# A feed-forward block whose four first products run ahead of its second products, with two PSUM banks taking turns

## The chip, the cores and the metric

The kernel runs on one core of a Trainium2 chip. A core has five engines with a queue of instructions each, worked off in order: TensorE (PE) multiplies matrices and writes to PSUM, VectorE (DVE), ScalarE (ACT) and GpSimd (POOL) work on elements, and SyncE (SP) issues DMA transfers. The metric is the device time of one execution in microseconds (us). Three timed runs of the kernel before took 1249.03, 1254.1 and 1255.2 us, the median is 1254.1. The profiled execution took 1257.39 us.

## The reference

Three stages, one after the other, on 4 batches of 576 tokens (2304 in all):

```
scores = q @ k.T / 8                          # 8 heads of 64, 576 keys
scores below a row's 32nd largest -> -1e9;  attn = softmax(scores);  x = attn @ v
h = x @ w_in                                  # 512 -> 2048
g = where(h > 0, h, exp(min(h, 0)) - 1);      x = g @ w_out        # 2048 -> 512
expert = argmax(cosine(x, expert_emb) / tau);  gate = its softmax weight
out = gate * (relu(x @ w1[expert]) @ w2[expert])                   # 8 experts, 512 -> 1024 -> 512
```

## The kernel before, in words

Numbers that need more than 16 bits are held as a high and a low half, so most products are three matmuls: high by high, high by low, low by high.

**Attention.** One tile is 128 queries of one head against 576 keys; four heads of the leftover 64 queries of a batch go in tiles of both heads together, so there are 144 tiles. PE makes the scores (line 781) into one of two score buffers of two PSUM banks each, ACT copies them out (787), DVE finds the threshold (676 to 708), ACT (691, 806, 818) and POOL (816, 821, 825) mask, exponentiate and split, SP transposes two tiles by DMA (827), and PE multiplies by v (857).

**Feed-forward.** After eight tiles 128 tokens are complete, which is a slot; there are 18. `norm_ops` divides by the sums, splits into two halves (`xs`, 889 to 895) and transposes by DMA to `xt`. `ffn_ops` then works in four units. A unit has a first product of 48 matmuls (`f1`, lines 916 to 918) into the PSUM bank `hp`; ACT takes exp and a clipped line of it (938, 939), DVE combines them with `hp` (940), and this is the last reader of the bank; ACT or POOL makes the high half `gt[0]` (945 or 943) and POOL the low half (946). The unit's second product is 12 matmuls of 512 columns (`f2`, 923 to 925) that add onto the PSUM bank `y`. Both products are issued in quarters (`K["cut"]` is 4), one operation of the planner each. When all four units have been added, `route_ops` takes `y` out of PSUM (962), turns it, finds the expert and its place in a list (966 to 1019), and writes the row to memory for the experts.

**Order.** A planner (`Plan`) writes the queues. Each operation has an engine, a supposed duration and a due time in tiles; an engine that is free takes, of the operations that can start, the one due first. The queue of each engine is fixed by this when the program is built. `Ring` hands out a set of buffers in turn, and a buffer is given again when the last user of its former holder is done. So with one `hp` bank the first product of unit 1 stands behind line 940 of unit 0. Eight PSUM banks are in use: `misc`, `sc` with four, `hp`, `y`, `acc`. There are two `gt` buffers and three `rr` buffers; `wl` is a 4 KB piece per partition through which the last of the feed-forward weights are prepared, and it is idle after that.

**Afterwards** the first expert's products on 128 early tokens start with the same two banks (`first_expert`), and then the experts run one by one behind a branch on a flag that all engines take.

Of the kernel before, what the change touches and what calls it, by code (L numbers as in the profile page):

```python
# [8 lines left out]
F32 = mybir.dt.float32  # L9
# [17 lines left out]
SC0 = 224  # L27

ENDS = (0, 83, 166, 248, 330, 412, 494, 576)
K = {'WD': 2.5, 'wa': 0.7, 'ws': 6.0, 'wsa': 0.6, 'wo': 6.0, 'wos': 13.0, 'wsp': (1, 1, 1, 1, 1, 1, 1, 1, 0, 0, 0, 0, 0, 0, 0, 0), 'kd': 5, 'qd': 7, 'vs': 1.3, 'va': 0.25, 'vp': -5.0, 'u': 20, 'cut': 4, 'ff0': 7, 'ffd': 7.0, 'rr': 3, 'nj': (3, 1), 'big': 3, 'kt': 4, 'wt': 0.4, 'wf': 0.9, 'vpo': 0, 'gth': 2, 'a4': (0, 20, 1), 'hp': 2, 'yb': 1, 'sc': 3, 'xt': 2, 'xsp': 0, 's': 5, 'w': 1, 'gt': 2, 'qraw': 1, 'dsc': 3.5, 'dcp': 2.0, 'dsg': 0.2, 'drl': 1.0, 'de': 1.0, 'dex': 0.8, 'dhi': 0.8, 'dlo': 0.9, 'dav': 3.5, 'dno': 3.5, 'drt': 2.0, 'f3': 0.3, 'f6': 0.6, 'f9': 0.9, 'f15': 2.4, 'ffs': 0.0, 'ct': 0.4, 'we': 0, 'wd0': -2.9, 'ahead': 4}  # L30


def pick(n, key):
# [156 lines left out]
def topk_attention_ffn_experts_kernel(  # L190
# [91 lines left out]
    def ring(pool, shape, dt, name, bufs):  # L282
        return Ring(bufs, lambda: pool.tile(shape, dt, name=name, bufs=bufs))
# [67 lines left out]
    def attention_and_ffn(fast):  # L351
# [30 lines left out]
        r_misc = ring(ps, [128, 512], F32, "misc", 1)  # L382

        r_sc = ring(ps, [128, 1024], F32, "sc", 2)
        r_h = ring(ps, [128, 512], F32, "hp", 1)
        r_y = ring(ps, [128, DM], F32, "y", K["yb"])
        r_acc = ring(ps, [128, DM], F32, "acc", 1)
        r_kraw = rings(raw, 2, ([128, NJ, 2, D], F32, "kraw"), ([64, 2, D], F32, "krawl"))
        r_vraw = rings(raw, 1, ([128, 2, NJ, D], F32, "vraw"), ([64, 2, D], F32, "vrawl"))
# [19 lines left out]
        r_xl = ring(at, [128, 2, DM], F16, "xl", 1)  # L409
        r_xt = ring(ff, [128, 2, KB, 128], F16, "xt", K["xt"])  # L410
        r_rr = ring(ff, [128, 512], F32, "rr", K["rr"])
        r_gt = ring(ff, [128, 2, 4, 128], F16, "gt", K["gt"])
        r_big = ring(ff, [128, 2 * S], F32, "big", K["big"])
        r_rt = rings(sm, 2, ([128, 5], F32, "ss"), ([128, 6, E], F32, "L"), ([128, 9], BF, "oh"), ([128, 2], I32, "pos"))
        r_pw = ring(sm, [128, 4], F32, "pw", 1)

        for r in [r_sc, r_s, r_k, r_php, r_pt, r_top, r_w, r_acc, r_xs, r_xt, r_h, r_gt, r_y]:
            r.in_order = True
        b_const = Buf(t=ident)
        b_sv, b_sw, b_so, b_sc3 = Buf(t=sv), Buf(t=sw), Buf(t=so), Buf(t=sc3)  # L420
# [78 lines left out]
        def w_split(t, tb, i, sb, due, pool):  # L499
            hi, lo, f = (wview(t, i, x) for x in range(3))  # L500
            s = sb.t[:, 0:1]
            if pool == 2:
                op("act", 1040, due, lambda: nc.scalar.activation(f, f, AF.Copy, scale=s), r=[sb], w=[tb[i + 1]])
                op("pool", 1105, due, lambda: nc.gpsimd.tensor_scalar(hi, f, 1.0, 0.0, op0=ALU.mult, op1=ALU.add), r=[tb[i + 1]], w=[tb[i]])
                op("pool", 2300, due, lambda: nc.gpsimd.tensor_tensor(lo, f, hi, op=ALU.subtract), r=[tb[i + 1]], w=[tb[i]])
                return
            op("act", 1040, due, lambda: nc.scalar.activation(hi, f, AF.Copy, scale=s), r=[tb[i + 1], sb], w=[tb[i]])
            if pool:
                op("act", 1040, due, lambda: nc.scalar.activation(f, f, AF.Copy, scale=s), r=[sb], w=[tb[i + 1]])
                op("pool", 2300, due, lambda: nc.gpsimd.tensor_tensor(lo, f, hi, op=ALU.subtract), r=[tb[i + 1]], w=[tb[i]])  # L510
                return
            op("dve", 1196, due, lambda: nc.vector.scalar_tensor_tensor(lo, f, s, hi, op0=ALU.mult, op1=ALU.subtract),
               r=[tb[i + 1], sb], w=[tb[i]])

        def wi_at(part, kb, fb):
            return wview(wi, fb // 2, part)[:, kb * 256 + (fb % 2) * 128:kb * 256 + (fb % 2) * 128 + 128]
# [2 lines left out]
            return wview(wo, fb // 2, part)[:, (fb % 2) * 512:(fb % 2) * 512 + 512]  # L519


        KT, VB, QT, hold = {}, {}, {}, []

        def thirds(x, m, first, due, dst, ns, reads):

# [88 lines left out]

        def get_q(b, j, due):
            n = 128 if j < NJ else SL
            x, m, qn, qd, qx = r_qraw(), (r_misc if QT else r_y)(), r_big(), r_qd(), Buf(t=1)
            QT[b, j] = qd
            op("sp", 750, due - 1.5, lambda: nc.sync.dma_start(x.t[:n], q[b, :, j * 128:j * 128 + n, :].rearrange("h p d -> p h d")),
               w=[x], lat=DLAT, after=hold if len(QT) > 1 else [])  # L620

            def part(i):
                return qn.t.bitcast(BF)[:, i * NP * 128:i * NP * 128 + NP * n]

            def tr():
                for p in range(NP):
                    turned(m.t[:, p * n:(p + 1) * n], x.t[:n, 2 * p:2 * p + 2, :].rearrange("p h d -> p (h d)"), n, p)

            def place():
                src = qn.t.bitcast(BF)[:, 0:3 * NP * 128].rearrange("p (i x) -> p i x", i=3)[:, :, 0:NP * n]  # L630
                for h in range(2):
                    rows = slice(64 * h, 64 * h + 64)
                    nc.sync.dma_start(qd.t[0:64, :, h, 0:NP * n], src[rows])
                    nc.sync.dma_start(qd.t[64:128, 0:2, h, 0:NP * n], src[rows, 0:2])
                    nc.sync.dma_start(qd.t[64:128, 2, h, 0:NP * n], src[rows, 0])

            op("pe", 430 if j < NJ else 270, due, tr, r=[x, b_const], w=[m, qn, qd])
            thirds(qx, m, NP * n, due - U, part, 478 if j < NJ else 290, [qn])
            op("sp", 2600, due - U, place, r=[qn, qx], w=[qd], lat=DLAT)
# [266 lines left out]


        def ffn_ops(c, d0, d1):
            xt, y = xts[c], r_y()

            def f1(hp, f, i0, i1):
                for i in range(i0, i1):
                    fb = 4 * f + i
                    for kb in range(KB):
                        xh, xl = (xt.t[:, x, kb, :] for x in range(2))
                        nc.tensor.matmul(hp.t[:, i * 128:i * 128 + 128], wi_at(0, kb, fb), xh, start=(kb == 0), stop=False)  # L916
                        nc.tensor.matmul(hp.t[:, i * 128:i * 128 + 128], wi_at(0, kb, fb), xl, start=False, stop=False)  # L917
                        nc.tensor.matmul(hp.t[:, i * 128:i * 128 + 128], wi_at(1, kb, fb), xh, start=False, stop=(kb == KB - 1))  # L918

            def f2(gt, f, i0, i1):  # L920
                for i in range(i0, i1):
                    fb = 4 * f + i
                    nc.tensor.matmul(y.t, gt.t[:, 0, i, :], wo_at(0, fb), start=(fb == 0), stop=False)  # L923
                    nc.tensor.matmul(y.t, gt.t[:, 0, i, :], wo_at(1, fb), start=False, stop=False)  # L924
                    nc.tensor.matmul(y.t, gt.t[:, 1, i, :], wo_at(0, fb), start=False, stop=(fb == NFB - 1))  # L925

            def unit(f):
                d = d0 + (d1 - d0) * f / (NFB // 4)
                hp, r, gt = r_h(), r_rr(), r_gt()
                n = 4 // K["cut"]  # L930

                def v3(x):
                    return x.rearrange("p (a b) -> p a b", a=4)

                for i in range(0, 4, n):
                    op("pe", 660 * n, d, lambda i=i: f1(hp, f, i, i + n), r=[xt] + wi_b[2 * f + i // 2:2 * f + (i + n + 1) // 2], w=[hp])

                op("act", 571, d + K["f3"], lambda: nc.scalar.activation(r.t, hp.t, AF.Exp, scale=sc3[:, 0:1]), r=[hp, b_sc3], w=[r])
                op("act", 707, d + K["f3"], lambda: nc.scalar.activation(r.t, r.t, AF.Relu, scale=sc3[:, 4:5], bias=sc3[:, 1:2]), r=[b_sc3], w=[r])
                op("dve", 720, d + K["f6"], lambda: nc.vector.scalar_tensor_tensor(r.t, hp.t, sc3[:, 2:3], r.t, op0=ALU.mult, op1=ALU.min),  # L940
                   r=[hp, b_sc3], w=[r])
                if (4 * c + f) * K["gth"] % 8 < K["gth"]:
                    op("pool", 588, d + K["f9"], lambda: nc.gpsimd.tensor_scalar(gt.t[:, 0], v3(r.t), 1.0, 0.0, op0=ALU.mult, op1=ALU.add), r=[r], w=[gt])
                else:
                    op("act", 520, d + K["f9"], lambda: nc.scalar.activation(gt.t[:, 0], v3(r.t), AF.Copy), r=[r], w=[gt])  # L945
                op("pool", 1113, d + K["f9"], lambda: nc.gpsimd.tensor_tensor(gt.t[:, 1], v3(r.t), gt.t[:, 0], op=ALU.subtract), r=[r], w=[gt])  # L946
                for i in range(0, 4, n):
                    FIRST["last"] = op("pe", 645 * n, d + K["f15"], lambda i=i: f2(gt, f, i, i + n), r=[gt] + wo_b[2 * f + i // 2:2 * f + (i + n + 1) // 2], w=[y])

            for f in range(NFB // 4):  # L950
                unit(f)
            route_ops(c, y, d1 + K["drt"])
            if c == NSLOT - K["ahead"]:
                first_tokens(d1 + K["drt"] + 1)
# [80 lines left out]
        def first_expert():  # L1035
# [6 lines left out]
            op("pool", 275, N + 3, lambda: nc.gpsimd.tensor_scalar(gate0, g.t[:, DM:DM + 1], 1.0, 0.0, op0=ALU.mult, op1=ALU.add), r=[g], w=[b_ids])  # L1042
            op("pe", 860, N + 3, lambda: turn0(m.t, g.t), r=[g, b_const], w=[m])
            op("act", 478, N + 3, lambda: nc.scalar.activation(x0, m.t, AF.Copy), r=[m], w=[x], after=old)
            up0(op, N + 60, x0, x, [r_h(), r_y()], late(0, 1024), Buf(t=1), raw, after=[FIRST["last"]])


        def start_ops():
# [450 lines left out]
```

## Time and profile before

| | us |
|---|---|
| median of 3 runs | 1254.1 |
| profiled execution | 1257.39 |
| its span in the trace | 1255.6 |
| busy in the span: PE, DVE, ACT, POOL | 1036.1, 865.1, 847.8, 780.8 |
| feed-forward and attention end at about | 938 |

Matmuls overlap in the trace and their ends are modelled, so that PE's busy time is an upper bound of what it needs. The stretches differ: the first 200 us prepare the weights, the stretch to 856 us is attention and feed-forward side by side, the next 80 us are what is left of feed-forward, and the last 317 us are the experts. Idle time of an engine counts only where another waits for it, so a row on a wait has to be read with the stretch in which it falls.

### The profile page before, as it was taken

The page shows a single profiled execution, that of the slowest core. Times are in us where ns is not written, and L with a number is a line of the kernel's source. Part 1 is how long each engine was busy: PE and PEld are TensorE (multiplying, and loading weights), DVE is VectorE, ACT ScalarE, POOL GpSimd, SP SyncE. Part 2 cuts the span into 40 slices and gives each one's busy share as a digit, 9 for nine tenths or more (in the row PEclk, how much of TensorE's full clock was granted, in tenths as well). Part 3 has the DMA queues.
Part 4 walks back from the last instruction along what each step waited for, and adds up shares of the span by engine and source line. Part 5 has one row for each costly group of instructions (what it writes and reads, how often), then busy time and mean ns, then how long its engine had stood idle before and what let it go on. Part 6 is the DMA issues. An engine that isn't in the chain of part 4 may idle for free. (4 is left out here: it accounts for less than half of the span.)

```text
span 1255.6 us, 28591 instructions
## 1 busy us (share of the span) xinstructions
PE 1036.1 (83%) x10112; PEld 799.0 (64%) x10112; DVE 865.1 (69%) x3588; ACT 847.8 (68%) x1807; POOL 780.8 (62%) x816
## 2 busy tenths in 40 slices
PE   4565537899798999798898988998887788998996
PEld 2354426666566777576676666776664677777785
DVE  4789999988798988789887898886213244434310
ACT  3687878889788989878887888876233244444421
POOL 1267979887688988678886788988313234323300
PEclk9957757999899999989998988999898889999998
DMA  7997633746764757945756674434407455455400
GB/s 202 303 235 192 161 93 71 144 94 149 161 122 100 125 107 156 167 81 102 126 95 127 146 145 85 90 77 89 136 11 228 143 184 185 134 163 178 142 20 16
DMA packets 321732, 165.85 MB, mean 132 GB/s; under 512 B 257990, under 2 KB 298054, under 8 KB 321552
## 3 DMA queue, kind: packets, MB, share of 16 engines
q1 hardware_dynamic: 316816, 150.67, 52.1%
q0 software_dynamic: 4736, 12.92, 3.4%
q8 instruction: 95, 1.56, 0.6%
q14 instruction: 85, 0.70, 0.2%
HBM read 77.43 MB, written 11.40 MB: 71 GB/s over the span
## 5 line engine op out<-in xcount | busy, mean ns | idle before, releaser
L916 PE MATMUL hp<-xt,ww 128*128 128x128 f16 x1152 | 216.8, 229 | 25.0 <-DVE rr L940 22.8
L917 PE MATMUL hp<-xt,ww 128*128 128x128 f16 x1152 | 216.7, 229 | 0.0
L918 PE MATMUL hp<-xt,ww 128*128 128x128 f16 x1152 | 216.4, 229 | 0.0
L816 POOL TENSOR_TENSOR arena<-arena,k 128x576 f32<-128x576 f32 x144 | 191.4, 1330 | 37.6 <-ACT k L806 36.7
L825 POOL TENSOR_TENSOR php<-arena,php 128x576 f16<-128x576 f32 x144 | 188.0, 1306 | 6.5
L781 PE MATMUL sc<-arena_r,qd 128*128 128x288 bf16 (+1 forms) x960 | 145.5, 308 | 43.2 <-ACT arena L787 17.7
L676 DVE MAX8 cand<-arena 128x8 f32<-128x82 f32 (+1 forms) x1008 | 161.3, 229 | 26.1 <-ACT arena L787 25.2
L787 ACT ACTIVATE arena<-sc 128x288 f32<-128x288 f32 x288 | 113.5, 408 | 47.0 <-PE sc L781 45.4
L857 PEld LDWEIGHTS <-pt 128*128 128x128 f16 (+3 forms) x2400 | 99.7, 104 | 68.6 <-DMA pt<-php 36.3
L781 PEld LDWEIGHTS <-qd 128*128 128x128 bf16 (+1 forms) x960 | 86.7, 107 | 88.4 <-issue 44.7
L916 PEld LDWEIGHTS <-ww 128*128 128x128 f16 x1152 | 119.8, 104 | 27.1 <-DVE rr L940 15.3
L821 POOL TENSOR_SCALAR php<-arena 128x576 f16<-128x576 f32 x144 | 101.5, 705 | 47.4 <-ACT arena L818 44.3
L917 PEld LDWEIGHTS <-ww 128*128 128x128 f16 x1152 | 118.8, 103 | 17.1 <-issue 11.9
L691 ACT ACTIVATE k<-arena,mba 128x576 bf16<-128x576 f32 x144 | 111.4, 774 | 14.8 <-DVE mx L696 7.7
L806 ACT ACTIVATE k<-arena,mba 128x576 bf16<-128x576 f32 x144 | 111.7, 776 | 14.0 <-DVE mba L708 8.0
L818 ACT ACTIVATE arena<-arena,mx 128x576 f32<-128x576 f32 x144 | 111.6, 775 | 11.8 <-POOL arena L816 11.4
L918 PEld LDWEIGHTS <-ww 128*128 128x128 f16 x1152 | 119.0, 103 | 0.0
L857 PE MATMUL acc<-vb,pt 128*128 128x64 f16 (+1 forms) x1920 | 91.5, 201 | 32.7 <-DMA pt<-php 30.8
L925 PE MATMUL y<-ww,gt 128*128 128x512 f16 x288 | 109.2, 379 | 4.6 <-POOL gt L946 4.6
L707 DVE MAX8 w<-w 128x8 f32<-128x585 f32 x144 | 109.9, 763 | 4.1 <-POOL w L701 3.2
L923 PE MATMUL y<-ww,gt 128*128 128x512 f16 x288 | 109.5, 380 | 0.6 <-ACT gt L945 0.6
L924 PE MATMUL y<-ww,gt 128*128 128x512 f16 x288 | 109.1, 379 | 0.0
(300 smaller groups left out, 2747.1 us busy)
## 6 DMA issues: line engine op xcount, KB each, us to landing
arena<-in_moe_w_dram SPq DMA_DIRECT2D x52, 512.0 KB, 5.6
arena_r<-big SPq DMA_DIRECT2D x64, 144.0 KB, 2.6
big<-in_moe_w_out_dram SPq DMA_DIRECT2D x16, 512.0 KB, 4.6
ww<-in_moe_w_in_dram SPq DMA_DIRECT2D x14, 512.0 KB, 7.1
qd<-big SPq DMA_DIRECT2D x32, 192.0 KB, 2.9
ysc<-big SPq DMA_DIRECT2D x20, 258.0 KB, 4.8
w<-in_moe_w_dram SPq DMA_DIRECT2D x10, 512.0 KB, 12.4
big<-in_v_dram SPq DMA_DIRECT2D x9, 512.0 KB, 8.8
```

The costliest lines, as they stand in the source:

```text
L676: v.max(out=cand.t[:, 8 * g:8 * g + 8], in_=x()[:, ENDS[g]:ENDS[g + 1]])
L691: op("act", 760, n + K["dsg"], lambda: nc.scalar.activation(k.t(), x(), AF.Sign, scale=-1.0, bias=th.t, accum_out=ds.t), r=[sb, th, k.base ...
L781: nc.tensor.matmul(o[64 * g:64 * g + 64] if s is None else o, qd.t[:, i, g, p * n:p * n + n], kt.t[:, g, i // 2, cs], start=i == 0, stop=i ...
L787: op("act", 291, n - K["dcp"], lambda c=c: nc.scalar.activation(sb.t()[:, c * 288:c * 288 + 288], sc.t[:, SC0 + c * 288:SC0 + c * 288 + 28 ...
L806: op("act", 667, n + K["drl"], lambda: nc.scalar.activation(k.t(), sb.t(), AF.Relu, scale=-HUGE, bias=kb.t), r=[sb, kb, s2, k2], w=[k])
L816: op("pool", 1242, e, lambda sb_=sb_, k_=k_: nc.gpsimd.tensor_tensor(sb_.t(), sb_.t(), k_.t(), op=ALU.subtract), r=[k_, s2, k2], w=[sb_])
L818: op("act", 760, e + K["dex"], lambda sb_=sb_, mx_=mx_, i_=i_: nc.scalar.activation(sb_.t(), sb_.t(), AF.Exp, scale=scale, bias=mx_(), acc ...
L825: op("pool", 1270, e + K["dlo"], lambda sb_=sb_, i=i: nc.gpsimd.tensor_tensor(ph.t[:, i, 1, 0:S], sb_.t(), ph.t[:, i, 0, 0:S], op=ALU.subt ...
L857: nc.tensor.matmul(acc.t[out_, cs], t[h][rows, g, :], rhs, start=(i == 0), stop=(i == len(units) - 1))
L916: nc.tensor.matmul(hp.t[:, i * 128:i * 128 + 128], wi_at(0, kb, fb), xh, start=(kb == 0), stop=False)
L917: nc.tensor.matmul(hp.t[:, i * 128:i * 128 + 128], wi_at(0, kb, fb), xl, start=False, stop=False)
L918: nc.tensor.matmul(hp.t[:, i * 128:i * 128 + 128], wi_at(1, kb, fb), xh, start=False, stop=(kb == KB - 1))
```

## The change

The first products of a slot's four units are issued with their elementwise work; the four activation results are kept in four `gt` buffers, two of which lie in `wl`; and the second products of all four follow, due close to the end of the slot's time. `hp` and `y` become one ring of two banks: of the five buffers that a slot takes, four are first products and the fifth is `y`. The writers of `gt` also wait for the last of the weight preparation (`done`), since that uses `wl`.

```diff
-        r_h = ring(ps, [128, 512], F32, "hp", 1)
-        r_y = ring(ps, [128, DM], F32, "y", K["yb"])
+        r_h = ring(ps, [128, 512], F32, "hp", 2)
...
-        r_gt = ring(ff, [128, 2, 4, 128], F16, "gt", K["gt"])
+        gts = [ff.tile([128, 2, 4, 128], F16, name=f"gt{i}", bufs=1) for i in range(2)]
+        gts += [wl.bitcast(F16)[:, i * 1024:i * 1024 + 1024].rearrange("p (a b c) -> p a b c", a=2, b=4) for i in range(2)]
+        r_gt = turns(4, lambda i: gts[i])
...
-            op("dve", 1196, due, lambda: nc.vector.scalar_tensor_tensor(lo, f, s, hi, op0=ALU.mult, op1=ALU.subtract),
-               r=[tb[i + 1], sb], w=[tb[i]])
+            done[:] = [op("dve", 1196, due, lambda: nc.vector.scalar_tensor_tensor(lo, f, s, hi, op0=ALU.mult, op1=ALU.subtract),
+               r=[tb[i + 1], sb], w=[tb[i]])]
...
-            xt, y = xts[c], r_y()
+            xt, second = xts[c], []
...
-                    op("act", 520, d + K["f9"], lambda: nc.scalar.activation(gt.t[:, 0], v3(r.t), AF.Copy), r=[r], w=[gt])
+                    op("act", 520, d + K["f9"], lambda: nc.scalar.activation(gt.t[:, 0], v3(r.t), AF.Copy), r=[r], w=[gt], after=done)
...
-                for i in range(0, 4, n):
-                    FIRST["last"] = op("pe", 645 * n, d + K["f15"], lambda i=i: f2(gt, f, i, i + n), r=[gt] + wo_b[2 * f + i // 2:2 * f + (i + n + 1) // 2], w=[y])
+                second.append((gt, f))
...
             for f in range(NFB // 4):
                 unit(f)
+            y, n = r_h(), 4 // K["cut"]
+            for gt, f in second:
+                for i in range(0, 4, n):
+                    FIRST["last"] = op("pe", 645 * n, d1 + (f - 3) * .2, lambda gt=gt, f=f, i=i: f2(y, gt, f, i, i + n),
+                                       r=[gt] + wo_b[2 * f + i // 2:2 * f + (i + n + 1) // 2], w=[y])
             route_ops(c, y, d1 + K["drt"])
...
-            up0(op, N + 60, x0, x, [r_h(), r_y()], late(0, 1024), Buf(t=1), raw, after=[FIRST["last"]])
+            up0(op, N + 60, x0, x, [r_h(), r_h()], late(0, 1024), Buf(t=1), raw, after=[FIRST["last"]])
```

The planner's order changes with it on all engines. First, TensorE's queue in the last slot, from the end of unit 1's first product on. The numbers behind the names tell allocations apart; `hp_15497` is unit 1's bank and `gt_15495` unit 0's result. Before:

```order
16085 L918 MATMUL hp_15497<-xt_15398,ww_151 128x128
16086 L923 LDWEIGHTS gt_15495
16087 L923 MATMUL y_15547<-ww_151,gt_15495 128x512
16088 L924 LDWEIGHTS gt_15495
16089 L924 MATMUL y_15547<-ww_151,gt_15495 128x512
```

Unit 1's first product is followed by unit 0's second. Now (`hp_15425` is unit 1's bank, `hp_15479` unit 2's, line numbers are larger by three):

```order
16083 L920 MATMUL hp_15425<-xt_15360,ww_151 128x128
16084 L921 LDWEIGHTS ww_151
16085 L921 MATMUL hp_15425<-xt_15360,ww_151 128x128
16086 L919 LDWEIGHTS ww_151
16087 L919 MATMUL hp_15479<-xt_15360,ww_151 128x128
```

Unit 2's first product stands at that place, in the other bank of the ring, and all the second products stand behind unit 3's first.

Second, GpSimd's queue where the last pair of attention tiles is finished (821 and 825 make its halves, 946 is the low half of a feed-forward unit of the last slot but one, 869 the sums). Before:

```order
L821 TENSOR_SCALAR php_114<-arena 128x576
L943 TENSOR_SCALAR gt<-rr 128x512
L825 TENSOR_TENSOR php_114<-arena,php_114 128x576
L946 TENSOR_TENSOR gt<-rr,gt 128x512
L821 TENSOR_SCALAR php_114<-arena 128x576
L869 TENSOR_SCALAR rinv<-sums 128x8
L825 TENSOR_TENSOR php_114<-arena,php_114 128x576
```

Now (lines 824, 828, 949 and 872 are the same four):

```order
L949 TENSOR_TENSOR gt_157<-rr,gt_157 128x512
L824 TENSOR_SCALAR php_114<-arena 128x576
L949 TENSOR_TENSOR wl<-rr,wl 128x512
L828 TENSOR_TENSOR php_114<-arena,php_114 128x576
L872 TENSOR_SCALAR rinv<-sums 128x8
L824 TENSOR_SCALAR php_114<-arena 128x576
L949 TENSOR_TENSOR wl<-rr,wl 128x512
L828 TENSOR_TENSOR php_114<-arena,php_114 128x576
```

Before, one low half of that slot stood ahead of the last attention product; now all four do.

Third, ScalarE's queue in slot 9 (938 is the exp of a unit, 939 its line, 945 its high half; 787, 691, 806 and 818 are attention). Before, from the third unit's exp on:

```order
L938 ACTIVATE rr<-hp,sc_125 128x512
L691 ACTIVATE k,dsa<-arena,mba 128x576
L939 ACTIVATE rr<-rr,sc_125 128x512
L818 ACTIVATE arena,sums<-arena,mx 128x576
L787 ACTIVATE arena<-sc 128x288
L818 ACTIVATE arena,sums<-arena,mx 128x576
L787 ACTIVATE arena<-sc 128x288
L527 ACTIVATE big<-misc 128x512
L945 ACTIVATE gt<-rr 128x512
L806 ACTIVATE k<-arena,mba 128x576
L527 ACTIVATE big<-misc 128x512
L787 ACTIVATE arena<-sc 128x288
```

Now (lines 941, 942 and 948 are the exp, the line and the high half; 694, 790, 809, 821 attention):

```order
L941 ACTIVATE rr<-hp,sc_125 128x512
L694 ACTIVATE k,dsa<-arena,mba 128x576
L942 ACTIVATE rr<-rr,sc_125 128x512
L790 ACTIVATE arena<-sc 128x288 x2
L809 ACTIVATE k<-arena,mba 128x576
L941 ACTIVATE rr<-hp,sc_125 128x512
L694 ACTIVATE k,dsa<-arena,mba 128x576
L821 ACTIVATE arena,sums<-arena,mx 128x576
L948 ACTIVATE wl<-rr 128x512
L942 ACTIVATE rr<-rr,sc_125 128x512
```

The third and fourth exp of a slot have moved together: five instructions lie between them now, and fifteen before (three more than the rows show).

## Rows read from the trace of the kernel before

**Rows 1.** The page's first line: span and instructions.
```profile
span 1255.6 us, 28591 instructions
```

**Rows 2.** Windows: start:end, length, busy us (count) of PE, PEld, DVE, ACT, POOL; PEclk; DMA.
```profile
200.00:856.00 656.00, 591.82 (x6992) 439.93 (x6992) 568.86 (x2746) 558.43 (x1279) 537.27 (x602) 0.95 0.61 119
856.00:892.00 36.00, 32.56 (x392) 24.23 (x390) 16.17 (x57) 18.94 (x37) 24.64 (x31) 0.95 0.59 153
938.00:1255.00 317.00, 266.00 (x1512) 223.83 (x1512) 102.64 (x170) 114.62 (x186) 87.23 (x66) 0.93 0.44 139
```

**Rows 3.** Waits, 200 to 856 us: who waited for whom; total us, times, longest.
```profile
ACT arena L787 <- PE sc L781: 34.2, 40, 3.8
DVE w L705 <- ACT k L691: 24.2, 32, 3.1
PE acc L857 <- DMA pt<-php: 20.9, 16, 4.0
PE hp L916 <- DVE rr L940: 12.6, 8, 5.9
```

**Rows 4.** Groups, 200 to 856 us: busy us, mean ns; idle before, releaser.
```profile
L787 ACT ACTIVATE arena<-sc 128x288 f32<-128x288 f32 x243 | 96.3, 409 | 35.8 <-PE sc L781 34.2
L806 ACT ACTIVATE k<-arena,mba 128x576 bf16<-128x576 f32 x122 | 94.7, 776 | 4.9 <-DVE mba L708 4.2
L818 ACT ACTIVATE arena<-arena,mx 128x576 f32<-128x576 f32 x122 | 94.6, 776 | 6.3 <-POOL arena L816 5.9
L691 ACT ACTIVATE k<-arena,mba 128x576 bf16<-128x576 f32 x122 | 94.6, 775 | 11.5 <-DVE mba L690 6.1 <-DVE mx L696 5.0
L925 PE MATMUL y<-ww,gt 128*128 128x512 f16 x244 | 92.5, 379 | 3.5 <-POOL gt L946 3.4
L946 POOL TENSOR_TENSOR gt<-rr,gt 128x512 f16<-128x512 f32 x62 | 73.0, 1177 | 4.2 <-ACT gt L945 3.4
L939 ACT ACTIVATE rr<-rr,sc 128x512 f32<-128x512 f32 x62 | 50.4, 813 | 0.3
L938 ACT ACTIVATE rr<-hp,sc 128x512 f32<-128x512 f32 x62 | 42.4, 684 | 12.2 <-PE hp L918 9.4 <-PE misc L975 2.4
L945 ACT ACTIVATE gt<-rr 128x512 f16<-128x512 f32 x47 | 29.5, 628 | 1.2 <-DVE rr L940 1.2
```

**Rows 5.** Waits of PE, 856 to 940 us.
```profile
PE hp L916 <- DVE rr L940: 5.4, 2, 2.9
PE y L925 <- POOL gt L946: 1.1, 2, 0.6
```

**Rows 6.** Timeline of PE, 891.8 to 898.1: start, us, instruction, idle before and releaser.
```profile
891.86 0.26 PE L857 MATMUL acc<-vbl,pt 64*128 64x64 f16 x3
...
897.94 0.27 PE L916 MATMUL hp<-xt,ww 128*128 128x128 f16 x1 [1.69 <-DMA xt<-xs]
```

**Rows 7.** Windows of PE alone: start:end, length, PE busy (count), PEclk, DMA.
```profile
870.40:875.00 4.60, 4.53 (x50) 0.63 0.65 125
897.90:904.90 7.00, 6.91 (x58) 0.52 0.00 0
907.30:911.60 4.30, 4.30 (x49) 0.60 0.04 4
911.60:914.20 2.60, 2.60 (x16) 1.00 0.00 0
914.20:916.85 2.65, 2.65 (x50) 1.00 0.00 0
911.60:929.03 17.43, 16.20 (x149) 1.00 0.00 1
```

**Rows 8.** Timeline of all engines, 904.8 to 907.3.
```profile
904.89 0.69 ACT L938 ACTIVATE rr<-hp,sc 128x512 f32<-128x512 f32 x1 [0.63 <-PE hp L918]
...
906.46 0.75 DVE L940 SCALAR_TENSOR_TENSOR rr<-hp,sc,rr 128x512 f32<-128x512 f32 x1 [1.73 <-ACT rr L939]
907.26 0.22 PE L916 MATMUL hp<-xt,ww 128*128 128x128 f16 x1 [2.41 <-DVE rr L940]
```

More of the change, by code (lines that the diff above doesn't have):

```diff
@@ L29 @@
 ENDS = (0, 83, 166, 248, 330, 412, 494, 576)
-K = {'WD': 2.5, 'wa': 0.7, 'ws': 6.0, 'wsa': 0.6, 'wo': 6.0, 'wos': 13.0, 'wsp': (1, 1, 1, 1, 1, 1, 1, 1, 0, 0, 0, 0, 0, 0, 0, 0), 'kd': 5, 'qd': 7, 'vs': 1.3, 'va': 0.25, 'vp': -5.0, 'u': 20, 'cut': 4, 'ff0': 7, 'ffd': 7.0, 'rr': 3, 'nj': (3, 1), 'big': 3, 'kt': 4, 'wt': 0.4, 'wf': 0.9, 'vpo': 0, 'gth': 2, 'a4': (0, 20, 1), 'hp': 2, 'yb': 1, 'sc': 3, 'xt': 2, 'xsp': 0, 's': 5, 'w': 1, 'gt': 2, 'qraw': 1, 'dsc': 3.5, 'dcp': 2.0, 'dsg': 0.2, 'drl': 1.0, 'de': 1.0, 'dex': 0.8, 'dhi': 0.8, 'dlo': 0.9, 'dav': 3.5, 'dno': 3.5, 'drt': 2.0, 'f3': 0.3, 'f6': 0.6, 'f9': 0.9, 'f15': 2.4, 'ffs': 0.0, 'ct': 0.4, 'we': 0, 'wd0': -2.9, 'ahead': 4}
+K = {'WD': 2.5, 'wa': 0.7, 'ws': 6.0, 'wsa': 0.6, 'wo': 6.0, 'wos': 13.0, 'wsp': (1, 1, 1, 1, 1, 1, 1, 1, 0, 0, 0, 0, 0, 0, 0, 0), 'kd': 5, 'qd': 7, 'vs': 1.3, 'va': 0.25, 'vp': -5.0, 'u': 20, 'cut': 4, 'ff0': 7, 'ffd': 7.0, 'rr': 3, 'nj': (3, 1), 'big': 3, 'kt': 4, 'wt': 0.4, 'wf': 0.9, 'vpo': 0, 'gth': 2, 'a4': (0, 20, 1), 'hp': 2, 'yb': 1, 'sc': 3, 'xt': 2, 'xsp': 0, 's': 5, 'w': 1, 'gt': 4, 'qraw': 1, 'dsc': 3.5, 'dcp': 2.0, 'dsg': 0.2, 'drl': 1.0, 'de': 1.0, 'dex': 0.8, 'dhi': 0.8, 'dlo': 0.9, 'dav': 3.5, 'dno': 3.5, 'drt': 2.0, 'f3': 0.3, 'f6': 0.6, 'f9': 0.9, 'f15': 2.4, 'ffs': 0.0, 'ct': 0.4, 'we': 0, 'wd0': -2.9, 'ahead': 4}
 def pick(n, key):
@@ L415, in attention_and_ffn @@
         r_pw = ring(sm, [128, 4], F32, "pw", 1)
-        for r in [r_sc, r_s, r_k, r_php, r_pt, r_top, r_w, r_acc, r_xs, r_xt, r_h, r_gt, r_y]:
+        for r in [r_sc, r_s, r_k, r_php, r_pt, r_top, r_w, r_acc, r_xs, r_xt, r_h, r_gt]:
             r.in_order = True
@@ L519, in wo_at @@
             return wview(wo, fb // 2, part)[:, (fb % 2) * 512:(fb % 2) * 512 + 512]
-        KT, VB, QT, hold = {}, {}, {}, []
+        KT, VB, QT, hold, done = {}, {}, {}, [], []
         def thirds(x, m, first, due, dst, ns, reads):
@@ L616, in get_q @@
             n = 128 if j < NJ else SL
-            x, m, qn, qd, qx = r_qraw(), (r_misc if QT else r_y)(), r_big(), r_qd(), Buf(t=1)
+            x, m, qn, qd, qx = r_qraw(), (r_misc if QT else r_h)(), r_big(), r_qd(), Buf(t=1)
             QT[b, j] = qd
@@ L918, in f1, with f2 @@
                         nc.tensor.matmul(hp.t[:, i * 128:i * 128 + 128], wi_at(1, kb, fb), xh, start=False, stop=(kb == KB - 1))
-            def f2(gt, f, i0, i1):
+            def f2(y, gt, f, i0, i1):
                 for i in range(i0, i1):
@@ L942, in unit @@
                 if (4 * c + f) * K["gth"] % 8 < K["gth"]:
-                    op("pool", 588, d + K["f9"], lambda: nc.gpsimd.tensor_scalar(gt.t[:, 0], v3(r.t), 1.0, 0.0, op0=ALU.mult, op1=ALU.add), r=[r], w=[gt])
+                    op("pool", 588, d + K["f9"], lambda: nc.gpsimd.tensor_scalar(gt.t[:, 0], v3(r.t), 1.0, 0.0, op0=ALU.mult, op1=ALU.add), r=[r], w=[gt], after=done)
                 else:
-                    op("act", 520, d + K["f9"], lambda: nc.scalar.activation(gt.t[:, 0], v3(r.t), AF.Copy), r=[r], w=[gt])
+                    op("act", 520, d + K["f9"], lambda: nc.scalar.activation(gt.t[:, 0], v3(r.t), AF.Copy), r=[r], w=[gt], after=done)
                 op("pool", 1113, d + K["f9"], lambda: nc.gpsimd.tensor_tensor(gt.t[:, 1], v3(r.t), gt.t[:, 0], op=ALU.subtract), r=[r], w=[gt])
-                for i in range(0, 4, n):
-                    FIRST["last"] = op("pe", 645 * n, d + K["f15"], lambda i=i: f2(gt, f, i, i + n), r=[gt] + wo_b[2 * f + i // 2:2 * f + (i + n + 1) // 2], w=[y])
+                second.append((gt, f))
             for f in range(NFB // 4):
                 unit(f)
+            y, n = r_h(), 4 // K["cut"]
[3 more added lines that the diff above has]
+                                       r=[gt] + wo_b[2 * f + i // 2:2 * f + (i + n + 1) // 2], w=[y])
             route_ops(c, y, d1 + K["drt"])
```

## The prediction

> **What bounds the kernel now.** I read the page first, then the windows, the waits, the groups, and at the end the timeline of the last slot. The span is 1255.6 us of an execution of 1257.4 [rows 1]. The windows cut it into stretches with different limits [rows 2]. From 200 to 856 us attention and feed-forward run side by side: PE is busy 592 of 656 us, DVE 569, ACT 558, POOL 537. No engine is full, none is idle; the four queues hold each other up. From 856 to 892 us DVE and ACT are busy 16 and 19 of 36 us and PE 33: the last scores are through, and PE works off feed-forward while the last attention tiles pass through POOL. From 892 to 938 PE alone matters, with the last slot. After that come 317 us of experts, which wait for this and which the change doesn't touch, so they move as a block.
>
> The wait that the change aims at is PE's first product behind line 940, the last reader of the one bank: 12.6 us in 8 waits between 200 and 856 us [rows 3], and 5.4 us in two waits after 856 [rows 5]. It isn't the largest. PE waits 20.9 us for transposed products, ACT 34.2 us for scores, DVE 24.2 us for ACT's line 691 [rows 3]. The timeline shows the mechanism without other work in it: unit 0's exp starts at 904.89, line 940 at 906.46, and the next first product at 907.26 [rows 8]. That is 2.4 us from the end of a first product to its bank being free.
>
> **The change part by part.** The number of matmuls, of elementwise instructions and of bytes stays as it is. What changes is order, banks and buffers.
>
> Term A, 200 to 856 us. What can go is the 12.6 us on line 940 and the 3.4 us in which PE waits for the low half of a result that it needs at once [rows 4]; four kept results take that away too. So 16.0 us is the one end. At the other end nothing goes: 5.9 us of the 12.6 is one wait [rows 3], in the first slot, when DVE still prepares weights, and a PE that waits less there only waits elsewhere. A gain in the middle needs that DVE, ACT and POOL follow, which are busy for 87, 85 and 82% [rows 2]. PE is the fullest engine by little, so I take a fifth of the 16.0 us: -3 us. What is late next is the transposed product, 20.9 us [rows 3], which the change doesn't shorten.
>
> By the Trainium skill, Perfetto Trace Analysis, section Identifying the Most-Contended Engine, matmul busy time misjudges how full TensorE is, and weight loads are to be read instead. PEld is busy 440 of 656 us, 67% [rows 2], less than any other engine; by that rule PE binds nothing in this stretch, term A is 0, and the sum would be 3 us higher.
>
> Term B, 856 to 892 us, from the last scores to the last product with v. PE loses 2.9 us here behind line 940 [rows 5] and runs the next first product at a granted clock of 0.63, its lower level for part of the time: 4.5 us where one takes 2.65 at 1.00 [rows 7]. Both go if unit 1 has its own bank: -2.9 - 1.9 = -4.8. Against this, 22 quarters of second products stand between the last scores and the last product with v in the new order, 20 in the old; a quarter is 2.60/4 = 0.65 us [rows 7], so +1.3. And POOL has all four low halves of slot 16 ahead of the last attention product instead of one (second pair of pieces of the order): 3 times 1.18 us [rows 4], +3.5, of which I count about half, since PE was the later one of the two before. Together -4.8 + 1.3 + 1.5 = -2. The ends are -4 and +4, the latter if POOL's extra work and its waits for units 1 to 3 come through in full.
>
> Term C, the last slot. Its input lands at 897.94, 5.8 us after the last product with v has ended at 892.12 [rows 6], and its last second product ends at 929.03: 31.1 us [rows 6, 7]. Nothing else is to be done meanwhile. In the old order the wait of 2.4 us [rows 8] comes after unit 0, unit 0 shares 7.0 us with the routing of slot 16, and the end has 1.2 us of waits for the results of unit 3 (17.43 - 16.20) [rows 7]. In the new order four first products come in a row and four second ones after them. The two banks suffice: a bank is free 2.4 us after its product [rows 8], and the product in between takes 2.65 us or more [rows 7]; `y` takes unit 2's bank, with unit 3 in between; and unit 3's result, another 0.63 + 1.18 us later [rows 4], has three second products of 2.60 us to come before it is wanted. The clock is the open part. The stretch from 897.9 ran at 0.52, and the next first product still at 0.60 with 4.3 us, after PE had waited for the input and again for the bank [rows 7]. I take two first products at 4.3 us and two at 2.65: 8.6 + 5.3 + 4 times 2.60 = 24.3 us, which is -6.8. With all four at the higher level it is 21.0, -10.1. With all at the lower it is 27.6, and if the 2.7 us of routing beside unit 0 (7.0 - 4.3) falls wholly before it, 30.3, -0.8.
>
> The first slot's results wait for the end of weight preparation, a new wait (`done`). Queued behind them on ACT and POOL is attention; but the planner starts unit 2 and 3 later for it, and the second products of that slot end at the same number of score tiles (32) in both orders, so I cost it at nothing; without that cover it would show as a later stretch from 200 us on, inside term A's ends.
>
> The sum is -3 - 2 - 6.8 = -11.8 us. From the profiled execution, 1257.4, that gives 1245.6; the median of the runs is 3.3 us lower, so 1242 us for the median after.
>
> **The rivals.**
>
> *Slower: ACT gets a slot's units in a lump.* The scores done between the start of unit 0's and the end of unit 3's first product were 9 tiles in slot 9 and are 3 now; the third pair of pieces of the order shows the exps moving together. A tile takes 656/122 = 5.4 us. ACT needs 558/122 = 4.6 us of it, of which feed-forward is 1.0 ((50.4 + 42.4 + 29.5)/122), so attention and the rest 3.6 [rows 2, 4]. Three tiles with a whole slot's units need 10.7 + 4 times (0.684 + 0.813) + 3 times 0.628 = 18.6 us in 16.1; four tiles need 22.2 in 21.5. That is 0.7 to 2.5 us too much in a slot, and DVE and POOL, which wait for ACT as it is [rows 3], would wait longer. At 1.4 us in 15 slots it costs 21 us, against 8.8 from B and C: +12, 1266 us. It decides the sign from 0.6 us a slot on. Against it: ACT has 98 us idle in the stretch [rows 2], and scores are made ahead of need, so a lump of 2 us can be made up in the five tiles that follow.
>
> *No change.* The waits move instead of going: PE stands behind the second bank, the score buffers or the transposed products (20.9 us already) and A is 0; POOL's extra halves make B +2; the clock stays low through C's first products, -4. That is -2, 1252 us. For it speaks that 34.2 us of ACT's waiting is for scores, which now stand behind longer runs of second products. Against it speaks C, which depends on little else.
>
> The Trainium skill, TensorE: Matmul & The Clock Gate, section HAM oscillation, reports a kernel that two PSUM buffers gave no further gain once TensorE was kept at work. By that rule A is 0 here, and only B and C are left.
>
> *More.* Half of the 16 us in A and the full clock in C: -8 - 2 - 10 = -20, 1234 us.
>
> **How the numbers follow.** Forecast 0.50, more 0.10, no change 0.24, slower 0.16. About 0.5%, 6.3 us, is what a measurement of this kernel can tell from no change. Faster by more than that (under 1247.8) is the forecast and the case of more, 0.60; within it 0.24; slower 0.16. The forecast's own range is 1235 to 1248: A from 0 to -8, C from -3.5 to -10. The range for 8 in 10 goes from 1231, since the lump rival can't make it faster and A's end of -16 is unlikely, to 1259, which leaves out most of the slower case.
>
> **What would show it.** After the change the waits of line 916's successor on line 940 should be near 0 in the last slot and under 4 us from 200 to 856; the last slot should take 22 to 27 us from its input to its last second product; the last product with v should end 0 to 4 us earlier in distance from the last scores; and the stretch to the last scores should be no longer. I am wrong if the last scores come later than 856 us by more than the tail gives back, with ACT's lines 691 and 806 as releasers of DVE and POOL grown, or if the last slot still takes 30 us because the clock stays low.

## The result

The changed kernel takes 1237.67 us in the median of four runs (1233.78 to 1243.32), the kernel before 1253.03 in the runs beside it; the ratio is 0.9893 with a 95% interval of 0.9864 to 0.9922. Six more runs later gave 0.9879 (0.9855 to 0.9904). Forecast were 1242 us and a range of 1231 to 1259. Ratios compare runs within 1.5% of the fastest of their kernel; medians in us are of all runs.

The page of the profile after, its first lines; columns of the second part are busy us, share of the span and instructions:

```profile
span 1241.5 us, 28592 instructions
PE 1032.4 (83%) x10112; PEld 791.5 (64%) x10112; DVE 864.4 (70%) x3588; ACT 845.2 (68%) x1807; POOL 777.7 (63%) x816
```

The span is 14.1 us shorter than before [rows 1]; the execution took 1243.32 us, before 1257.39. All five busy times are within 1% of what they were. So little became cheaper, and most of the 14 us is waiting that went. The windows say where. Columns as before: start:end, length, busy us of PE, PEld, DVE, ACT, POOL, then PEclk and DMA:

```profile
200.00:851.40 651.40, 592.71 (x6915) 433.24 (x6914) 572.15 (x2753) 557.12 (x1280) 535.02 (x603) 0.95 0.62 119
851.40:887.00 35.60, 33.21 (x403) 23.60 (x400) 13.78 (x57) 20.43 (x41) 26.99 (x37) 1.00 0.57 115
```

The last scores are through at 851.5 us, before at 855.9. In the next stretch PE's clock is 1.00, where it was 0.95 [rows 2]: PE stops for a bank once, for 0.5 us, where it was 2.9. The waits of the long stretch, 200 to 851.4 us (total us, times, longest), with line numbers larger by three than before:

```profile
ACT arena L790 <- PE sc L784: 40.0, 44, 4.8
DVE cand L679 <- ACT arena L790: 20.2, 27, 4.0
PE acc L860 <- DMA pt<-php: 14.7, 13, 2.9
DVE w L708 <- ACT k L694: 13.4, 28, 1.5
PE sc L784 <- DVE mba L693: 10.4, 1, 10.4
```

The first product's wait for the last reader of its bank (12.6 us [rows 3]; the reader is now line 943) is no longer in the list by that name. What is left shows in three groups: line 919 begins a first product, and lines 926 and 928 are in a second one, whose bank now comes from the same ring:

```profile
L919 PE MATMUL hp<-xt,ww 128*128 128x128 f16 x960 | 171.4, 223 | 2.4 <-DMA xt<-xs 1.2 <-DVE mba L693 1.1
L926 PE MATMUL hp<-ww,gt 128*128 128x512 f16 x128 | 51.8, 404 | 4.8 <-DVE mba L693 2.7 <-DVE rr L943 1.3 <-DVE top L689 0.8
L928 PE MATMUL hp<-ww,gt 128*128 128x512 f16 x128 | 51.4, 402 | 1.0 <-POOL gt L949 1.0
```

The name behind an arrow is only the last event before the start. Line 926 at 393.20 us started 0.05 us after a line 943 had ended, though its row names line 693. So up to 5.9 us of waits for a bank are left, 4.8 at line 926 and 1.1 at line 919; one more, of 4.5 us in the first slot, ended at 191.4 us, ahead of the window, as one of 4.8 us did before. For a low half a second product now waits 1.0 us (3.4 before [rows 4]).

One wait is new. In the first slot the scores wait 10.4 us, until 210.5, and start 0.05 us after line 706, the last reader of a score buffer, which stands on DVE behind the preparation of weights (line 515). Before, a first product stood 5.9 us for its bank there, also behind DVE's preparation of weights. PE's idle time in the whole stretch fell from 64.2 to 58.7 us.

PE's wait for transposed products fell from 20.9 to 14.7 us and DVE's for line 691 (now 694) from 24.2 to 13.4. Not all was gained: ACT waits 40.0 instead of 34.2 us for scores [rows 3], which stand behind longer runs of second products, and DVE twice as long as before for ACT's copies of them, 20.2 us.

The end of feed-forward on PE's timeline (start, us, instruction, idle before and its releaser):

```profile
885.48 0.26 PE L860 MATMUL acc<-vbl,pt 64*128 64x64 f16 x3
...
887.66 1.32 PE L977 MATMUL misc<-ent,rr 128*128 128x8 f32 x8 [1.34 <-ACT rr L1004]
890.36 0.17 PE L981 MATMUL misc<-oh,tri 128*128 128x8 bf16 x1 [1.38 <-DVE oh L1013]
892.76 0.27 PE L919 MATMUL hp<-xt,ww 128*128 128x128 f16 x1 [2.20 <-DMA xt<-xs]
```

and its windows, PE alone (length, busy, PEclk, then DMA share and GB/s):

```profile
885.70:892.70 7.00, 2.13 (x16) 0.69 1.11 344
892.76:906.35 13.59, 13.59 (x193) 0.79 0.12 42
906.35:916.83 10.48, 10.48 (x51) 1.00 0.01 2
```

The last slot's input is there at 892.76, the four first products take 13.6 us without a gap, the four second ones 10.5: 24.1 us, before 31.1. The second products run at 1.00 throughout; the first begin after 7 us in which PE worked for 2.1, and their clock is 0.79 on average.

With the ends of the stages read from PE's timelines, in us (the last row counts the experts to the span's end):

| stage | before | after | difference |
|---|---|---|---|
| to the last scores | 855.9 | 851.5 | -4.4 |
| from there to the last product with v | 36.2 | 34.3 | -1.9 |
| from there to the last slot's first product | 5.8 | 7.0 | +1.2 |
| last slot, first to last product | 31.1 | 24.1 | -7.0 |
| the rest | 326.6 | 324.7 | -1.9 |

### The profile page after: what moved, and what is told of

It reads as the page before. It is cut to its first block, busy times and chain, and to the rows that moved or that the text cites. A ratio compares the mean times of both kernels' runs of the same rounds, so it can differ in the third digit from the quotient of the medians.

```text
span 1241.5 us, 28592 instructions
## 1 busy us (share of the span) xinstructions
PE 1032.4 (83%) x10112; PEld 791.5 (64%) x10112; DVE 864.4 (70%) x3588; ACT 845.2 (68%) x1807; POOL 777.7 (63%) x816
## 5 line engine op out<-in xcount | busy, mean ns | idle before, releaser
L919 PE MATMUL hp<-xt,ww 128*128 128x128 f16 x1152 | 210.1, 225 | 9.6 <-DVE less L702 4.5
L920 PE MATMUL hp<-xt,ww 128*128 128x128 f16 x1152 | 209.8, 225 | 0.0
L921 PE MATMUL hp<-xt,ww 128*128 128x128 f16 x1152 | 209.5, 225 | 0.0
L784 PE MATMUL sc<-arena_r,qd 128*128 128x288 bf16 (+1 forms) x960 | 148.2, 314 | 48.8 <-DMA arena_r<-big 14.6
L784 PEld LDWEIGHTS <-qd 128*128 128x128 bf16 (+1 forms) x960 | 88.6, 109 | 95.1 <-issue 36.2
L860 PEld LDWEIGHTS <-pt 128*128 128x128 f16 (+3 forms) x2400 | 97.1, 103 | 59.0 <-DMA pt<-php 30.2
L919 PEld LDWEIGHTS <-ww 128*128 128x128 f16 x1152 | 116.9, 101 | 11.8 <-DVE less L702 4.6
L920 PEld LDWEIGHTS <-ww 128*128 128x128 f16 x1152 | 116.3, 101 | 9.7 <-issue 5.0
L921 PEld LDWEIGHTS <-ww 128*128 128x128 f16 x1152 | 116.4, 101 | 0.0
L706 DVE SCALAR_TENSOR_TENSOR w<-sc,mba,arena 128x576 f32<-128x576 f32 x124 | 100.6, 811 | 0.2
L689 DVE MAX8 top<-cand 128x8 f32<-128x56 f32 x432 | 88.3, 210 | 3.0
L1333 DVE SCALAR_TENSOR_TENSOR hl<-hp,hh 128x256 fp32r<-128x256 f32 x56 | 23.1, 421 | 96.3 <-ACT hh L1332 96.3
## 6 DMA issues: line engine op xcount, KB each, us to landing
w<-in_moe_w_dram SPq DMA_DIRECT2D x10, 512.0 KB, 10.5
```

Of the source, the lines that this page charges most:

```text
L784: nc.tensor.matmul(o[64 * g:64 * g + 64] if s is None else o, qd.t[:, i, g, p * n:p * n + n], kt.t[:, g, i // 2, cs], start=i == 0, stop=i ...
L860: nc.tensor.matmul(acc.t[out_, cs], t[h][rows, g, :], rhs, start=(i == 0), stop=(i == len(units) - 1))
```

## The experiments

The theory was that the second bank pays, in the last slot and, less, in the long stretch. The rivals were that the four kept results or the late second products pay; and, after the first four runs, that the long stretch only depends on the particular order which the planner happens to write.

**One bank each, the rest as changed.**

```diff
-        r_h = ring(ps, [128, 512], F32, "hp", 2)
+        r_h = ring(ps, [128, 512], F32, "hp", 1)
+        r_y = ring(ps, [128, DM], F32, "y", 1)
...
-            y, n = r_h(), 4 // K["cut"]
+            y, n = r_y(), 4 // K["cut"]
```

> The changed kernel with four kept results and the late due times, but with one bank for first products and one for y, as before. Theory (the second bank is what pays): each first product stands behind line 940 of the unit before again, the last slot takes 29 to 32 us from its input to its last second product (24.1 with two banks), and the time is back within 4 us of the kernel before, ratio 0.997 to 1.003. Rival (the late second products and the four kept results pay): the ratio stays at 0.987 to 0.992.

Measured: ratio 1.0027 (1.0003 to 1.005). The last slot took 31.1 us, and on PE's timeline of it the wait is back:

```profile
908.51 0.23 PE L920 MATMUL hp<-xt,ww 128*128 128x128 f16 x1 [2.54 <-DVE rr L944]
```

The planner fills the time behind a bank with second products, as in the kernel before. In this one order, four kept results and late due times alone are worth nothing.

**The last slot alone, and all slots but the last.** In both, `hp` and `y` are two rings of one bank; slots in `NEW` take them in turn, the others as before.

```diff
+        NEW, at_bank = set([17]), [0]          # the other kernel: set(range(17))
...
+                if old:
+                    for i in range(0, 4, n):
+                        FIRST["last"] = op("pe", 645 * n, d + K["f15"], lambda i=i: f2(y, gt, f, i, i + n), ...
+                else:
+                    second.append((gt, f))
```

> Two banks in turn and second products in one go in the last slot alone; the 17 slots before it as in the kernel before (four result buffers everywhere). Theory: the last slot takes 24 to 25 us instead of 31.1, and of the 14 us between the two kernels 5 to 8 come, ratio 0.994 to 0.996. Rival (the gain is spread over the stretch to the last scores): at most 3 us, ratio 0.998 or more.

Measured: 0.9974 (0.9945 to 1.0003). The last slot took 25.2 us, close to what was expected; but the last product with v ended at 900.9 us in the profile, against 892.1, although 17 slots kept the old structure. The four result buffers and the wait for `done` stand in those slots too, and the planner's order came out another one there. The profiled execution was also a long one, 1260.0 us against a median of 1251.5, so that part of the 8.8 us is spread.

> The counterpart: two banks in turn and second products in one go in slots 0 to 16, the last slot with one bank and a second product after each first, as before. Theory: what the last slot gave (6 to 7 us) is missing and the 4 to 6 us of the stretches before it are there, ratio 0.994 to 0.997. Rival (a changed order makes luck in the long stretch, nothing lasting): ratio 0.998 to 1.005.

Measured: 1.0019 (0.9986 to 1.0052). The last slot took 28.1 us and the last product with v ended at 895.2. The two parts together give -0.07%, the whole -1.1 to -1.2%. The theory's range for the total missed in both runs, and in the second the rival's range came: the size of the last slot was right in the first, and in the long stretch the order moved more than the part that was tested. That made the rival of the order the one to test.

**Two result buffers.**

```diff
-        r_gt = turns(4, lambda i: gts[i])
+        r_gt = ring(ff, [128, 2, 4, 128], F16, "gt", 2)
```

> The changed kernel with two result buffers instead of four. Theory: a result is wanted 10 us after its unit, but the third only needs the first second product done, and unit 3 follows closely; in the last slot two buffers cost 0 to 2 us, in the long stretch 0 to 5, ratio 0.989 to 0.995. Rival (the four kept results are what takes the waits away): the waits of second products for the low half come back, the gain is lost, ratio 0.997 or more.

Measured: 1.0001 (0.9965 to 1.0036); the theory's expectation missed, the rival's came. The last slot took 22.7 us, so two buffers do there. Its profiled execution was a long one, 1266 us against a median of 1259, so I take no other stage times from it. One wait of its long stretch isn't in either other kernel's list at that size (3.4 us in 7 waits before, 6.7 us in 7 after):

```profile
POOL gt L947 <- ACT gt L946: 15.3, 9, 5.8
```

POOL stands behind a high half that ACT has not made yet. That the high half in turn waits for a free result buffer is argued from the code, not shown. In this order the gain is gone without the kept results, as it went without the second bank in the first run. That both are needed in any order isn't shown: each was left out in one order only, and an order alone moves as much, as the last runs below show.

**The same order again, and the clock.** The first is the changed kernel itself.

> The changed kernel once more, unchanged, with more runs, since the partial kernels gave less than expected. Theory: 0.987 to 0.992 again, the last slot at 24 us. Rival (the first measurement, of four runs, was lucky): 0.993 to 0.998, which is what the last slot alone is worth.

Measured: 0.9879 (0.9855 to 0.9904), last slot 24.0 us. The first measurement was no luck.

```diff
             def f1(hp, f, i0, i1):
+                if c == NSLOT - 1 and f == i0 == 0:
+                    warm(34)
...                                        # and warm(18) ahead of each of the two routing products of slot 16
```

> The changed kernel with 70 idle matmuls (128 columns, into an unused part of a score bank) put into the three gaps of TensorE between the last product with v and the last slot's first product; the rest of the order is the same. Theory (the first products of the last slot start at the lower clock since PE idled): they take 10.6 to 11.5 us instead of 13.6, the time falls by 2 to 3 us against the changed kernel. Rival (the idle matmuls delay the routing or the input's transfer): first products start later by 1 us or more and nothing is gained.

Measured: 0.9873 (0.9838 to 0.9908), 1238.94 us beside 1239.61 of the changed kernel; the two can't be told apart by their times, so the expected fall of 2 to 3 us isn't shown. The trace is clear. PE alone in the gap, in the four first products and in the four second:

```profile
885.00:891.90 6.90, 5.85 (x87) 1.00 1.11 351
891.90:902.70 10.80, 10.78 (x192) 1.00 0.15 55
902.70:913.20 10.50, 10.50 (x52) 1.00 0.00 0
```

The clock stays at 1.00, and the four first products take 10.8 instead of 13.6 us. The last slot took 21.3 us. So the lower clock cost 2.8 us, and it came from the idle time before it. This version is 2.7 us better where it was changed and no worse elsewhere that could be seen.

**Other orders of both structures.** If the order alone made the gain, other orders of the new structure would lose it, and some of the old would reach it.

```diff
-                    FIRST["last"] = op("pe", 645 * n, d1 + (f - 3) * .2, ...
+                    FIRST["last"] = op("pe", 645 * n, d1 - .5 + (f - 3) * .2, ...
```

> The changed kernel with the second products due half a tile earlier: the same structure, but another order in the long stretch. Theory (the two banks and late second products pay in the long stretch by themselves): ratio 0.987 to 0.993. Rival (the long stretch depends on the particular order, by more than the change is worth there): last slot at 24 to 25 us as in the changed kernel, last scores 4 us or more later, ratio 0.993 to 1.005.

```diff
-                d = d0 + (d1 - d0) * f / (NFB // 4)
+                d = d0 + (d1 - d0) * f / (NFB // 4) / 4
```

> The changed kernel with the first products of a slot due within 1.3 tiles instead of 5.3, so that their elementwise work comes to ACT and POOL in an even closer lump. Theory (ACT has room and a lump costs little): ratio 0.984 to 0.994. Rival (a lump costs 0.7 to 2.5 us a slot, the slower case of the prediction): the last scores 10 us or more later than in the changed kernel, DVE waiting longer for ACT's line 691 and its copies, ratio 0.996 or more.

In the other four only a number of the table `K` is changed: `drt` from 2.0 to 2.6 in the changed kernel and in the kernel before, and `f15` from 2.4 to 2.2 and to 2.7 in the kernel before.

> The changed kernel with the routing of a slot due 0.6 of a tile later: a third order of the new structure. Theory: 0.986 to 0.993, the last slot at 21 to 25 us. Rival (the changed kernel's order is lucky in the long stretch): 0.994 to 1.002, last product with v later than 892 us.

> The kernel before with the same shift of the routing, 0.6 of a tile later: a fourth order of the old structure, the counterpart of the run before it. Theory: 0.998 to 1.008, the last slot at 31 us. Rival: 0.994 or less.

> The kernel before with its second products due 0.2 of a tile earlier: the old structure in another order, as a measure of what an order alone moves. Theory: within 4 us of the kernel before, ratio 0.997 to 1.003. Rival (the particular order matters): the last scores come more than 4 us earlier or later, ratio outside 0.997 to 1.003 either way, with the last slot at 31 us unchanged.

> The kernel before with its second products due 0.3 of a tile later: a third order of the old structure. Theory (the old structure loses to the new one whatever its order): 0.998 to 1.008. Rival (one order in a few reaches what the changed kernel does): 0.992 or less.

Measured, with the stages from one profile each:

| kernel | ratio, 95% interval | last scores | last product with v ends | last slot |
|---|---|---|---|---|
| before | 1 | 855.9 | 892.1 | 31.1 |
| before, `f15` 2.2 | 1.0064 (1.0041 to 1.0087) | 872.9 | 907.0 | 31.2 |
| before, `drt` 2.6 | 1.0078 (1.0049 to 1.0106) | 860.0 | 893.7 | 30.7 |
| before, `f15` 2.7 | 1.0110 (1.0084 to 1.0136) | 872.1 | 906.8 | 30.6 |
| after | 0.9893 (0.9864 to 0.9922) | 851.5 | 885.7 | 24.1 |
| after, again | 0.9879 (0.9855 to 0.9904) | 848.6 | 883.9 | 24.0 |
| after, second products earlier | 0.9906 (0.9875 to 0.9938) | 860.3 | 889.9 | 23.2 |
| after, first products in a lump | 0.9915 (0.9888 to 0.9942) | 850.0 | 888.5 | 23.0 |
| after, `drt` 2.6 | 0.9915 (0.9890 to 0.9941) | 846.5 | 881.9 | 24.0 |

An order alone moves the old structure by up to 1.1%, so the order does matter as much as the change. But the two groups don't overlap: four orders of the new structure lie between 0.988 and 0.992, four of the old between 1.000 and 1.011. The gain isn't the luck of one order; the old kernel's order was the best of its four. The rival that an order explains all is refuted for these eight, and the expectation for the old structure with `f15` 2.2, that a shift stays within 0.3%, missed, as did the one for `f15` 2.7 (0.998 to 1.008). With the second products earlier the rival's sign came, last scores 8.8 us later than in the changed kernel, but not its ratio. The last scores of the two groups overlap, the ends of the last product with v don't. Which of the second bank, the kept results and the late second products pays in the long stretch, these runs don't tell.

The lump answers the slower case of the prediction. From a slot's first exp on ACT to its fourth it was 29.7 us before, 20.3 in the changed kernel and 15.9 here (mean of slots 1 to 15 in the traces). In this closer lump DVE's waits for ACT, 200 to 850 us, are

```profile
DVE cand L679 <- ACT arena L790: 19.7, 29, 3.9
DVE w L708 <- ACT k L694: 15.2, 30, 1.6
```

35 us together, as in the changed kernel (33.6) and in the kernel before (24.2 and 10.4). No loss from the lumps shows.

## Why the prediction was right

**Term A, the long stretch, -3.** The profile gives -4.4 to the last scores, and in the second profile of the same kernel they come at 848.6, -7.3. Of the 16.0 us of waits for a bank and for low halves some 9 went; 5.9 and 1.0 are left. That a PE which waits less in the first slot only waits elsewhere came true: 5.9 us behind DVE's preparation of weights became 10.4. PE's idle time fell by 5.5 us. The fifth that I took was low. That PE binds nothing here and the term is 0, which the prediction drew from how full weight loads are (the Trainium skill, Perfetto Trace Analysis, section Identifying the Most-Contended Engine), isn't borne out by these two profiles: weight loads are busy 67% as before, and the stretch is shorter. The size of this term isn't well defined: the planner's order moves this stretch by as much, and I had no row for that. The kernel before is the best of its four orders. Against the mean of all four (899.9 us in the table) the new ones end the last product with v 13.6 us earlier (886.3, the changed kernel's two profiles counted as one), where A and B make 5.

**Term B, -2.** Measured -1.9. That it fits to 0.1 us is luck: the stretch took 35.3 us in the second profile of the same kernel (34.3 in the first), 29.6 to 38.5 in the other new orders and 33.7 to 34.8 in the other old ones. Of its parts the lower clock went as worked out, and of the wait 0.5 us is left:

```profile
PE hp L919 <- DVE rr L943: 0.5, 1, 0.5
PE acc L860 <- DMA pt<-php: 1.0, 1, 1.0
```

(waits of PE, 851 to 930 us). The second row is POOL's extra work: the last product with v now waits for its transposed input, where before it stood behind second products only. POOL's last attention half ended 26.9 us after the last scores, before 20.0.

**Term C, -6.8.** Measured -7.0. Worked out were 13.9 us of first products and 10.4 of second, measured 13.6 and 10.5. The fit of the first products is in part luck. Two were taken at 4.3 us and two at 2.65; they took 5.08, 3.02, 2.68 and 2.85 us at clocks of 0.50, 0.88, 1.00 and 1.00, so the first was longer and the second shorter than worked out. The run with idle matmuls showed the lower clock as the cause of what they took above 10.8, and its last slot of 21.3 us is near the 21.0 worked out for all four at the higher level. Their start was 1.2 us later after the last product with v than before; this was not in the sum. It came from the transfer: the halves of the last input were ready 2.6 us after that product in both kernels, and from the issue of the transposing transfer to the first product it then took (PE's windows, before and after; the last two columns are DMA share and GB/s)

```profile
894.77:897.94 3.17, 0.70 (x5) 0.99 0.43 83
888.39:892.76 4.37, 0.79 (x5) 0.50 1.12 341
```

In the 14 profiles this took 3.1 to 3.7 us where the DMA share was 0.74 or less, and 3.9 to 7.7 us where it was 0.94 or more. That the weights of the experts, which are loaded at that time, hold it up is argued from this.

**What the sum lacked** is the 1.9 us by which the experts' part was shorter. Its length was between 320.6 and 328.4 us in the twelve other profiles, so this is spread, and not the change.

**The rivals.** The lump at ACT was wrong: DVE's waiting for ACT at lines 679 and 708 stayed at 34 us, only its place changed; at line 943, which waits for ACT's clipped line, it grew from 6.0 to 11.6 us, and the stretch was still shorter. That all waits would only move instead of going is half true: ACT's wait for scores grew by 6 us and DVE's for the copies by 10, while DVE's for line 691 fell by 11 and PE's for transposed products by 6. That a second bank makes term A 0, which the prediction drew from the report of one kernel (the Trainium skill, TensorE: Matmul & The Clock Gate, section HAM oscillation), isn't settled: without the second bank the last scores came at 862.3 us and the ratio is 1.0027, but in one order. In the last slot the second bank is worth 7 us.

## What to carry to other kernels

Where one accumulator is filled in turns with the products that feed it, issue all feeding products first and let both banks take turns; in the long stretch neither the second bank nor the place to keep every result paid alone, in the one order in which each was tried, and in the last slot the bank paid with two results as well. Look at the end of the kernel first: there one engine works alone, the sum can be made from rows, and it came true to 0.2 us here, though two errors on the clock offset each other in it. Before a gain of a per cent in a long stretch of coupled queues is put down to a change, measure a few other orders of both versions: here an order alone was worth 1.1%.

## What the runs showed that I had not expected

TensorE's clock could be kept at 1.00 through a wait of 7 us by 70 small matmuls of no use in its gaps, and the first products behind it ran in 10.8 instead of 13.6 us. And small shifts of a due time, 0.2 or 0.3 of a tile, cost the old kernel 0.6 and 1.1% with the same number of matmuls and elementwise instructions.
